# Keys' first part on ScalarE, row sums in halves, stores from another queue, output jobs placed later

## The chip, the cores and the metric

The kernel runs on one core of a Trainium2 chip, as one launch. The metric is the device time of that launch in microseconds (us), lower being better. Five engines work side by side, each through its own instructions in order: TensorE (PE), VectorE (DVE), ScalarE (ACT), GpSimd (POOL) and SyncE (SP), which here only issues DMA transfers. An instruction that waits holds up everything behind it on its engine. PE writes its results into PSUM banks, which other engines must empty before PE can use them again.

## The reference

```python
def _attn_ref(q, k, v, cap):                 # 4 batches, 12 heads, 448 rows, 64 wide
    scores = scale * np.matmul(q, k.transpose(0, 1, 3, 2))
    scores = cap * np.tanh(scores / cap)
    scores = scores - np.max(scores, axis=-1, keepdims=True)
    attn = np.exp(scores)
    attn = attn / (np.sum(attn, axis=-1, keepdims=True) + 1e-09)
    return np.matmul(attn, v)

def _moe_ref(x, modality_id, w_gate, modality_bias, w1, w2):   # 1792 x 768, 8 experts, 1024 wide
    logits = x @ w_gate + modality_bias[modality_id]
    e_idx = np.argmax(logits, axis=1)
    ...                                      # gate_w: the softmax weight of the chosen expert
    for e in range(E):
        mask = e_idx == e
        h = np.maximum(x[mask] @ w1[e], 0.0)
        out[mask] = gate_w[mask, None] * (h @ w2[e])

def _moe2_ref(x, w_gate, w_val, w_out):      # 768 -> 1536 -> 768
    gate = 1.0 / (1.0 + np.exp(-(x @ w_gate)))
    val = x @ w_val
    return gate * val @ w_out
```

The three run one after the other: attention, a layer in which each row goes to one expert, and a gated layer.

## The kernel before

All large products run in float16 with each operand split into a high part and a low part (the rest), so that three matmuls of parts stand for one product. Making the parts is work for ACT and DVE: `split_hi` (L923) copies the high part on ACT, line 928 subtracts it on DVE or POOL.

**Attention.** Heads are taken in pairs, six pairs a batch, 24 in all. A pair has four steps over keys (j = 0 to 3): `qk` makes scores, ACT takes tanh (L300) and exp (L305), `av` multiplies with values, and DVE adds up the rows for the sum (L325, L327, L333). The operands of the next pair are made beside it: `trans_k` in step 0 and `trans_q` in step 1 transpose on PE into a PSUM bank that `tr_tile` hands out. Then `parts_of` makes the high part (L259 on DVE, or L257 on ACT) and the low part (L260 on DVE), which frees the bank. Keys' parts are both made on DVE, queries' high part on ACT. One or two banks serve all these transposes and those of the ends of a batch, `end0g` to `end2`, L415 among them. Between them DVE converts weights of the gated layer for later (`conv_ops`, L862 to L864).

**Experts.** Rows are sorted into blocks of 128 by expert; the profile shows 15 blocks (540 matmuls at L730, 36 a block). Step s of the loop multiplies block s by w1 (`mm1`), applies relu on ACT (L734), transposes the result (`trh`, L709 on PE, L711 on ACT, L712 on DVE), multiplies block s-1 by w2 in two halves (`mm2`, L749), and takes that result out of its bank on ACT and DVE (`put_y`, L757, L758). A block of a new expert has its weights split by `split_w` (L689 on ACT, L693 on DVE) inside a branch, for w1 after relu (`split_new`) and for w2 after `put_y` (`next_w2`). A step has three places for other work, `fill[0]` to `fill[2]`. There go conversions of weights from `CV["raw"]` to `CV["cvt"]`, and in `fill[2]`, after `put_y`, the row sums: `y_sums(0, p)` makes for a tile of two blocks (p = 0 to 3) the sums of quarters that the seven-product scheme below needs. It returns four parts, a, b, d and e; DVE works at L975 to L1000, ACT copies the high part of each sum (L923), DVE makes the low one (L978). Tile 0's sums stand in step 9, those of tiles 1 and 2 in steps 10 and 11, inside a branch on the number of blocks (true here). After `fill[2]` come the jobs in `M["due"]`: from step 6 to 12 `set_keep` stores the two converted tiles from `CV["cvt"]` to DRAM (`keep`, L892, on SP's queue). The next step's conversions write those tiles again.

**The gated layer.** Each matrix product is made on two-by-two blocks with seven products instead of eight (Strassen's scheme in Winograd's form). The work has two halves (`sup` 0 and 1: eight and six tiles of 128 rows). In each, twelve sets of weights run through `gset`, then the output product runs in pieces of two tiles: p = 0 to 3 in the first half, 0 to 2 in the second. `z_job` makes a piece's seven operands: sums on DVE (`sums_of`, L901, two functions s1 and s2) and for each of the seven a high part on ACT and a low part on DVE (in the second half in turns on DVE and POOL), L920. Piece p+1's operands are made while piece p multiplies; `ZAT` and `ZBT` say after which product of that piece each job is issued, and `work` issues product and jobs in that order. A number past the last product means after the last.

A product is followed by what empties its bank (`opiece`). In `chain` four of the seven products add into one bank, one after the other, and after each ACT copies it (L1137). DVE adds the rest (L1140). In piece 0 and in the second half's last piece the seven have banks of their own (`seven`) and ACT copies one. A finished tile is sent to the output by an indirect DMA from POOL (L1126). The second half's rows come back through transposing DMAs on SP's queue (`y_load(1, ...)`, L966) into the space that pieces 0 and 1 read from. Their sums `y_sums(1, p)` run beside pieces 2 and 3 (`QC`, `QB`).

Of the kernel before, what the change touches and what calls it, by code (L numbers as in the profile page):

```python
# [57 lines left out]
WL = (0, 0, 0, 11, 25, 40)  # L58
FIRST = [(0, 1), (0, 2), (0, 7), (0, 6), (1, 1), (0, 5), (1, 2), (1, 6), (0, 3), (0, 4)]
QA = (6,) * 16  # L60
QB = (0, 1, 1, 2, 2, 3, 4, 4)
QC = (2, 3, 4, 5)
ZAT = (7, 7, 8, 8, 9, 9, 10, 10, 11)
ZBT = (0, 0, 0, 1, 1, 2, 3, 5, 6)

AFTER = ({'g0': 1, 'g1': 1, 's': 1, 'e1s': 4, 'e1g': 5, 'route': 6, 'route_b': 8, 'ga': 9, 'gb': 10, 'gc': 12, 'sc': (10, 12, 14, 16), 'e2': (7, 10, 12, 17, 21, 24), 'xw': (26, 27)}, {'g0': 1, 'g1': 1, 's': 1, 'e1s': 4, 'e1g': 5, 'route': 6, 'route_b': 10, 'ga': 9, 'gb': 10, 'gc': 12, 'sc': (10, 12, 14, 16), 'e2': (7, 10, 12, 17, 20, 23), 'xw': (26, 27)}, {'g0': 1, 'g1': 1, 's': 1, 'e1s': 5, 'e1g': 5, 'route': 6, 'route_b': 7, 'ga': 10, 'gb': 11, 'gc': 13, 'sc': (10, 11, 12, 13), 'e2': (6, 9, 10, 11, 12, 13), 'xw': (15, 15), 'ta': (9, 9), 'w1': (11, 11, 14, 12, 13, 13), 'w1s': (17, 18, 19, 23, 24, 24), 'w1l': (17, 18, 19, 26, 26, 26), 'idx': (11, 11), 'gather': (17, 18, 25), 'trx': (24, 25), 'w2': (20, 21, 26, 26)})

# [2 lines left out]
def tile_kernel(ctx: ExitStack, tc: tile.TileContext, q, k, v, cap, mod, wg, mb, w1, w2, gw, vw, ow, out, dbg=None):  # L70
    nc = tc.nc
# [176 lines left out]
    def tr_tile():  # L248

        M["trs"].append(M["trs"].pop(0))  # L250
        return bank(M["trs"][-1], "tr")

    def parts_of(dst, pt, n, eng):

        hi, lo = dst[:, 0], dst[:, 1]
        if eng is nc.scalar:
            nc.scalar.activation(out=hi, in_=pt[:, :n], func=AF.Copy, scale=SQ)  # L257
        else:
            eng.tensor_scalar(out=hi, in0=pt[:, :n], scalar1=SQ, scalar2=None, op0=ALU.mult)  # L259
        nc.vector.scalar_tensor_tensor(out=lo, in0=pt[:, :n], scalar=SQ, in1=hi, op0=ALU.mult, op1=ALU.subtract)  # L260

    def trans_k(g):

        b, i = divmod(g, NPAIR)
        t = kT[g] = att.tile([128, 2, 512], F16, name="kT")
        pt = tr_tile()
        for c in range(3):
            nc.tensor.transpose(pt[:, 128 * c:128 * c + 128], kf[g][:, c].rearrange("p h d -> p (h d)"), id32)
        nc.tensor.transpose(pt[:, 384:512], kt[b % 2][:, i], id32)
        parts_of(t, pt, 512, nc.vector)  # L270

    def trans_q(g):
        t = qT[g] = att.tile([128, 2, S], F16, name="qT")
# [560 lines left out]
    CV = {}  # L834
# [35 lines left out]
    def set_raw(s):  # L870
        for e in range(2):
            conv_load(*unit(s, e), CV["raw"][e])

    def wo_raw(i):
        for e in range(2):
            conv_load(2, 2 * i + e, CV["raw"][e])
# [4 lines left out]
    def g32_of(s, e):  # L881
        kind, j = unit(s, e)
        r = 128 * (12 * kind + j)
        return g32[r:r + 128, :]

    def set_keep(s):

        for e in range(2):
            keep(s, e)

    def keep(s, e):
        nc.sync.dma_start(out=g32_of(s, e), in_=CV["cvt"][e])  # L892

    def set_load(s, tiles):
        for e in range(2):
# [38 lines left out]
    def wo_job(t, w, to):  # L934

        s1, s2 = sums_of(False, t, w)
        ops = operands(False, t, w)
        hi, lo = splits([(ops[p], (to[:, p - 1, 0], to[:, p - 1, 1]), nc.vector) for p in (1, 2, 3, 5, 6, 7, 4)])
        return [s1, s2] + hi + lo
# [226 lines left out]
    with tc.manual_schedule():  # L1166
# [83 lines left out]
        for n in range(4 * NG + LAG):  # L1250
            g, j = divmod(n, 4)
# [111 lines left out]
            Z["wa"] = pool("wap", side="right").tile([128, 7, 2, 3, 128], F16, name="wa")  # L1363

        Z["ct"] = lambda s: CV["cvt"]
        M["due"] = []

        wst = [yr[:, c:c + 14 * 384].rearrange("p (q a n) -> p q a n", q=7, a=2) for c in (0, 12 * 512, 24 * 512)]
# [5 lines left out]
                    rest(s + 1)  # L1374

        YT = {8: 3, 9: 4, 10: 5, 12: 6, 13: 7}
        YS, YF = (9, 10, 11), (2, 2, 2)

        def y_more(p, cond):
            with tc.If(cond):  # L1380
                for f in y_sums(0, p):
                    f()

        def y_rest(tiles, cond):
# [3 lines left out]
        def conv_fill(fill, units):  # L1388

            c = [conv_ops(u[0], CV["raw"][e], CV["cvt"][e]) for e, u in enumerate(units)]  # L1390
            fill[0].extend(c[0][:3])
            fill[1].extend((c[0][3],) + c[1][:3])
            fill[2].append(c[1][3])

        for s in range(2, NFULL):
            fill = [], [], []
            i = s - WFILL
            if 0 <= i < NWO:
                conv_fill(fill, [(2, 2 * i + e) for e in range(2)])
                fill[1].append(lambda i=i: wo_raw(i + 1) if i + 1 < NWO else set_raw(early_sets[0]))  # L1400
                fill[2].extend(wo_job(halves(*CV["cvt"]), Z["w"], wst[i]))
            if 0 < i <= NWO:
                M["due"].append(lambda i=i: nc.sync.dma_start(out=wod[i - 1], in_=wst[i - 1].rearrange("p q a n -> p (q a n)")))
            if FILL <= s < FILL + len(early_sets):
                n = early_sets[s - FILL]
                conv_fill(fill, [unit(n, e) for e in range(2)])
                M["due"].append(lambda n=n: set_keep(n))
                if n != early_sets[-1]:
                    fill[1].append(lambda n=early_sets[s - FILL + 1]: set_raw(n))
                if n == 0:  # L1410
                    fill[2].extend(set_job(0, (nc.vector,) * 7))

            t = {5: 0, 6: 1, 7: 2}.get(s)
            if t is not None:
                fill[0].append(lambda t=t: y_load(0, (t,)))
            if s == YS[0]:
                fill[2].extend(y_sums(0, 0))
            if s == 6:

                nc.scalar.activation(out=M["glast"], in_=padc, func=AF.Sigmoid)  # L1420
            if s == 8:

                few = nc.values_load(tabs["b"][1][0:1, 0:1], engines=[ENG.SP], min_val=NFULL, max_val=NSLOT)
                fewv = nc.values_load(tabs["b"][1][0:1, 0:1], engines=[ENG.DVE, ENG.Activation, ENG.Pool], min_val=NFULL, max_val=NSLOT)
            for p in (1, 2):
                if s == YS[p]:
                    fill[YF[p]].append(lambda p=p: y_more(p, fewv < 16))
            t = YT.get(s)
            if t is not None:
                fill[0].append(lambda t=t: y_rest((t,), few < 16))  # L1430
            if s == 12:
                fill[0].append(lambda: y_rest((3,), few > 15))
            if s == 13:
                fill[2].append(lambda: y_more(1, fewv > 15))
            step(s, fill, more if s == 2 else None)
# [92 lines left out]

        def zjobs(sup, p, bufs, tmps, whole):
            j = z_job(sup, p, bufs, tmps, (DV, GP, DV, GP, DV, GP, DV) if sup else (DV,) * 7, allp, whole)  # L1530
            return list(zip(ZAT if p == 1 else ZBT, j))

        def work(calls, jobs):

# [7 lines left out]

            return [old[0], new[0], old[1], *new[1:], *old[2:]] if old else new

        pend = []
        for sup in range(2):
            nt = (4, 3)[sup]
            reg = (yr.bitcast(F32), zr)[sup]
# [3 lines left out]
            for s in range(12):  # L1552
                jobs = []
                if s < 11:
                    j = set_job(s + 1, LO[sup]) if sup or s else job
# [27 lines left out]
                pend = [prod(s, p) for p in (5, 7, 3, 4)]  # L1583
                work(calls, jobs)
            for p in range(nt):
                whole = p == 0 or sup and p == nt - 1
                jobs = []
                if p == 0:
                    jobs += [(6, f) for f in z_job(sup, 0, z0, zt, (DV,) * 7, slice(5, 6))]
                if sup == 0 and p == 2:  # L1590
                    Z["ct"] = lambda s: stg[2 * (s % 2):2 * (s % 2) + 2]
                    jobs += [(0, lambda: y_load(1, range(8, 14)))]
                    jobs += [(1, lambda: [set_load(s, Z["ct"](s)) for s in range(2)])]
                if p + 1 < nt:
                    jobs += zjobs(sup, p + 1, zbufs[p + 1], zt, sup and p + 1 == nt - 1)
                if sup == 0 and p == 2:
                    jobs += zip(QC, y_sums(1, 0))
                    jobs += zip(QA, set_job(0, (DV,) * 7))
                if sup == 0 and p == 3:
                    jobs += zip(QB, [f for i in range(1, 3) for f in y_sums(1, i)])  # L1600
                mm = opiece(sup, p, zbufs[p], whole)
                if p == 0:

                    calls = [lambda q_=q_, ks=ks, mm=mm: mm(q_, ks=ks) for ks in (range(5), range(5, 6)) for q_ in OORD]
                elif whole:
                    calls = [lambda q_=q_, mm=mm: mm(q_) for q_ in OORD]
                if whole:
                    calls = mixed(calls[:3], pend) + calls[3:]
                    pend = []
                else:  # L1610
                    calls = mixed([lambda q_=q_, mm=mm: mm(q_) for q_ in (1, 2, 6)], pend)
                    pend = [lambda q_=q_, mm=mm: mm(q_) for q_ in (5, 7, 3, 4)]
                work(calls, jobs)
# [40 lines left out]
```

## Time and profile before

| | us |
|---|---|
| median of 3 runs | 987.41 |
| lowest and highest run | 986.48, 987.56 |
| the profiled execution, its own time | 989.69 |
| its span, first to last instruction | 987.8 |
| PE busy in it | 922.4 |
| DVE, ACT, POOL busy | 710.2, 506.0, 172.3 |

The rows below come from that one execution. Its own time is 1.9 us more than its span. A row of a timeline has the start from the span's beginning, the duration, the engine, the line of the kernel, the operation, what is written from what, the shape, and how many instructions were merged into the row. In brackets stands how long the engine was idle before it and what ended that. "q" after an engine is its sequencer, which branches, waits and issues DMAs. "PE L749 <- DVEq L813" is a wait that DVE ended.

### The profile page before, as it was taken

Reading aid. Unit: us, or ns where it says so; the run is one execution under the profiler, and the core shown is the slowest. Engines: PE = TensorE matmul, PEld = TensorE weight load, DVE = VectorE, ACT = ScalarE, POOL = GpSimd, SP = SyncE. Lnnn points to the kernel's source line nnn. Section 1 sums busy time; section 2 is a strip of 40 time slices with the busy share of each in tenths; the row PEclk is TensorE's granted clock in tenths of the full one; section 3 lists DMA queues with packets and bytes.
Section 4 is the critical chain, followed back from the end, with each engine's and each line's share of the span. In section 5 each row is a group of like instructions: output and inputs, shape, how many; then the busy total and the mean of one; then the engine's idle time right before and its main releaser. Section 6 shows DMA issues by size and latency. Waiting matters only on the chain. (4 is left out here: it accounts for less than half of the span.)

```text
span 987.8 us, 14820 instructions
## 1 busy us (share of the span) xinstructions
PE 922.4 (93%) x5291; PEld 473.6 (48%) x5291; DVE 710.2 (72%) x1239; ACT 506.0 (51%) x817; POOL 172.3 (17%) x221
## 2 busy tenths in 40 slices
PE   6998989989898999989797999999989899999996
PEld 2333333333455555555355444444556556666554
DVE  4879888687774995387944899996698744545661
ACT  6978768658214663244532666544354345554330
POOL 4000000001011121111110000000010178883131
PEclk9999999989999999999999999999999999999999
DMA  5634464436347568759440555231062122220001
GB/s 137 168 99 113 115 189 117 124 101 230 129 126 301 187 220 267 235 171 373 161 130 20 159 197 181 96 117 43 17 126 83 65 96 81 79 67 1 1 33 64
DMA packets 119787, 128.78 MB, mean 130 GB/s; under 512 B 74464, under 2 KB 99952, under 8 KB 118928
## 3 DMA queue, kind: packets, MB, share of 16 engines
q1 hardware_dynamic: 114688, 107.83, 35.5%
q0 software_dynamic: 4208, 19.66, 5.8%
q8 instruction: 44, 0.72, 0.3%
q14 instruction: 47, 0.39, 0.1%
q10 hardware_dynamic: 800, 0.20, 0.1%
HBM read 91.16 MB, written 30.99 MB: 124 GB/s over the span
## 5 line engine op out<-in xcount | busy, mean ns | idle before, releaser
L1044 PEld LDWEIGHTS <-wa 128*128 128x128 f16 x909 | 89.6, 99 | 86.4 <-issue 8.3
L749 PE MATMUL sc<-w2s,hs 128*128 128x384 f16 x720 | 123.6, 329 | 6.8 <-DVEq L813 4.9
L730 PE MATMUL sc<-w1s,xT 128*128 128x512 f16 x540 | 120.0, 379 | 2.4 <-DVE w1s L693 1.5
L1044 PE MATMUL pp<-yr,wa 128*128 128x512 f16 (+1 forms) x468 | 101.3, 372 | 6.2 <-DVEq L1372 4.7
L749 PEld LDWEIGHTS <-hs 128*128 128x128 f16 x720 | 71.0, 99 | 49.6 <-ACT sta L865 5.2
L300 ACT ACTIVATE E<-sc,sct 128x896 f32<-128x896 f32 x72 | 72.4, 1006 | 41.5 <-PE sc L292 40.4
L730 PEld LDWEIGHTS <-xT 128*128 128x128 f16 x540 | 52.7, 98 | 64.4 <-issue 2.2
L1044 PE MATMUL pp<-zr,wa 128*128 128x384 f16 x441 | 75.7, 326 | 0.6 <-ACT yr L1092 0.6
L305 ACT ACTIVATE E<-E,capt 128x896 f32<-128x896 f32 x72 | 74.7, 1038 | 0.6
L314 PE MATMUL ot<-E,vf 128*64 128x448 f32 x288 | 70.3, 569 | 0.2 <-ACT E L305 0.2
L1044 PE MATMUL pp<-wos,yr 128*128 128x384 f16 x378 | 63.5, 331 | 5.7 <-ACT hs L1137 5.7
L901 DVE TENSOR_TENSOR sta<-sta 128x384 f32<-128x384 f32 x108 | 67.3, 663 | 2.0 <-DVE sta L901 0.5
L1126 POOL DMA_INDIRECT out_dram<-hs,pm x14 | 14.6, 1044 | 265.7 <-DVE hs L1140 198.7
L292 PE MATMUL sc<-qT,kT 64*128 64x448 f16 x432 | 56.1, 367 | 1.2 <-DVE kT L259 1.0
L1044 PEld LDWEIGHTS <-wb 128*128 128x128 f16 x378 | 37.0, 98 | 34.5
L1044 PEld LDWEIGHTS <-yr 128*128 128x128 f16 x378 | 37.5, 99 | 31.7 <-issue 8.1
L923 ACT ACTIVATE wa<-sta 128x384 f16<-128x384 f32 x98 | 48.6, 513 | 7.4 <-DVE sta L901 4.1
L1074 DVE TENSOR_TENSOR yr<-yr,pp 128x384 f32<-128x384 f32 x24 | 13.3, 553 | 46.4 <-PE pp L1044 46.4
L1044 PE MATMUL pp<-yr,wb 128*128 128x512 f16 x189 | 43.9, 379 | 0.0
L712 DVE TENSOR_TENSOR xT<-tr,xT 128x384 f16<-128x384 f32 x34 | 17.2, 551 | 34.7 <-ACT xT L711 34.3
L1024 PE MATMUL pp<-wos,sta 128*128 128x384 f16 x252 | 41.9, 326 | 0.0
L928 POOL TENSOR_TENSOR wa<-sta,wa 128x384 f16<-128x384 f32 x42 | 39.8, 965 | 6.0 <-ACT wa L923 6.0
(314 smaller groups left out, 1596.2 us busy)
## 6 DMA issues: line engine op xcount, KB each, us to landing
sta<-g SPq DMA_DIRECT2D x40, 384.0 KB, 3.1
st<-in_moe_w_dram SPq DMA_DIRECT2D x8, 1536.0 KB, 9.7
sta<-in_moe_w_out_dram SPq DMA_DIRECT2D x12, 768.0 KB, 4.4
sta<-in_moe_w_val_dram SPq DMA_DIRECT2D x12, 768.0 KB, 4.5
g<-sta SPq DMA_DIRECT2D x18, 384.0 KB, 4.4
qf<-in_q_dram SPq DMA_DIRECT2D x48, 112.0 KB, 3.9
vf<-in_v_dram SPq DMA_DIRECT2D x24, 192.0 KB, 2.9
st<-in_moe_w_gate_dram SPq DMA_DIRECT2D x6, 768.0 KB, 5.5
```

The costliest lines, as they stand in the source:

```text
L292: nc.tensor.matmul(sc[:, h, :S], kt_[p, a, 128 * j:128 * j + 128], qt_[p, b_], start=i == 0, stop=i == 2)
L300: nc.scalar.activation(out=e, in_=src, func=AF.Tanh, scale=sct)
L305: nc.scalar.activation(out=e, in_=e, func=AF.Exp, scale=capt)
L314: nc.tensor.matmul(ot[g][64 * h:64 * h + 64, :S], vf[g][:, h, j], e[:, h], start=j == 0, stop=False)
L712: nc.vector.tensor_tensor(out=lo, in0=pt[:, :128 * n], in1=hi, op=ALU.subtract)
L730: nc.tensor.matmul(p[:, nh], xT[s % 2][:, a, kk], w1s[:, b_, kk, 512 * nh:512 * nh + 512], start=i == 0, stop=i == 17)
L749: nc.tensor.matmul(M["p2"][:, nh, :384], hT[par][:, a, kk], w2s[:, b_, kk, 384 * nh:384 * nh + 384], start=i == 0, stop=i == 23)
L901: tt = lambda eng, o, x, y, op: eng.tensor_tensor(out=o, in0=x, in1=y, op=op)
L923: nc.scalar.activation(out=hi, in_=src, func=AF.Copy)
L928: los = [lambda x=x, d=d, e=e: e.tensor_tensor(out=d[1], in0=x, in1=d[0], op=ALU.subtract) for x, d, e in todo]
L1024: nc.tensor.matmul(bk[p][:, c0:c1], l(p, a, kk), r(p, b_, kk)[:, c0:c1], start=i == 0, stop=i == 3 * kn - 1)
L1044: nc.tensor.matmul(bk[c][:, c0:c1], l(p, a, kk), r(p, b_, kk)[:, c0:c1], start=i == c0 == 0 and p in (1, 2, 7), stop=i == 3 * kn - 1 and c ...
```

## The change

Four things change. `trans_k` has keys' high part made on ACT for the first five pairs of batches 1 to 3, 15 pairs. `keep` issues its stores from ACT's queue in the block loop, 14 stores. The row sums of tiles 0, 1 and 2 are cut in two, parts a and b in one step and d and e in the next, in steps 7 to 12 instead of 9 to 11; those of tiles 1 and 2 take two branches each. In the output stage, piece 1's second sums s2 are issued after piece 0's last product and the three jobs behind it (`carry`) after piece 1's first. Of piece 2's jobs the first three are issued after piece 1's first product and the other six after its third, behind the copy that follows that product. The row sums beside piece 3 start one product later.

```diff
-QB = (0, 1, 1, 2, 2, 3, 4, 4)
+QB = (1, 2, 2, 3, 4, 4, 5, 6)
 QC = (2, 3, 4, 5)
-ZAT = (7, 7, 8, 8, 9, 9, 10, 10, 11)
+ZAT = (7, 7, 8, 8, 9, 17)
 ZBT = (0, 0, 0, 1, 1, 2, 3, 5, 6)
+ZCT = (0, 0, 0, 2, 2, 2, 2, 2, 2)
...
-        parts_of(t, pt, 512, nc.vector)
+        parts_of(t, pt, 512, nc.scalar if b and i < 5 else nc.vector)
...
     def keep(s, e):
-        nc.sync.dma_start(out=g32_of(s, e), in_=CV["cvt"][e])
+        (nc.scalar if CV.get("own") else nc.sync).dma_start(out=g32_of(s, e), in_=CV["cvt"][e])
...
         Z["ct"] = lambda s: CV["cvt"]
+        CV["own"] = True
         M["due"] = []
...
-        YS, YF = (9, 10, 11), (2, 2, 2)
-
-        def y_more(p, cond):
+        YS = {7 + 2 * p + i: (p, slice(2 * i, 2 * i + 2)) for p in range(3) for i in range(2)}
+
+        def y_more(p, cond, which=slice(0, 4)):
             with tc.If(cond):
-                for f in y_sums(0, p):
+                for f in y_sums(0, p)[which]:
                     f()
...
-            if s == YS[0]:
-                fill[2].extend(y_sums(0, 0))
...
-            for p in (1, 2):
-                if s == YS[p]:
-                    fill[YF[p]].append(lambda p=p: y_more(p, fewv < 16))
+            if s in YS:
+                p, which = YS[s]
+                if p:
+                    fill[2].append(lambda p=p, which=which: y_more(p, fewv < 16, which))
+                else:
+                    fill[2].extend(y_sums(0, 0)[which])
...
             j = z_job(sup, p, bufs, tmps, (DV, GP, DV, GP, DV, GP, DV) if sup else (DV,) * 7, allp, whole)
-            return list(zip(ZAT if p == 1 else ZBT, j))
+            if p == 1:
+                carry.extend((0, f) for f in j[6:])
+            return list(zip(ZAT if p == 1 else ZCT if p == 2 else ZBT, j))
...
-        pend = []
+        pend, carry = [], []
...
-                jobs = []
+                jobs, carry[:] = carry[:], []
```

## Rows read from the trace of the kernel before

**Rows 1.** The page, busy time of each engine, share of the span, instructions.
```profile
PE 922.4 (93%) x5291; PEld 473.6 (48%) x5291; DVE 710.2 (72%) x1239; ACT 506.0 (51%) x817; POOL 172.3 (17%) x221
```

**Rows 2.** Timeline of all engines, 49 to 53 us, around one pair's keys.
```profile
49.31 0.67 ACT L305 ACTIVATE EM<-EM,capt 128x448 f32<-128x448 f32 x1
...
50.39 1.01 ACT L300 ACTIVATE E<-sc,sct 128x896 f32<-128x896 f32 x1 [0.42 <-PE sc L292]
...
50.85 0.68 DVE L259 TENSOR_SCALAR kT<-tr 128x512 f16<-128x512 f32 x1
...
51.56 0.69 DVE L260 SCALAR_TENSOR_TENSOR kT<-tr,kT 128x512 f16<-128x512 f32 x1
...
52.36 0.57 PE L276 MATMUL tr<-id,qf 112*128 112x112 f32 x4 [1.10 <-issue]
```

**Rows 3.** PE's timeline, 190 to 216 us: the last of the seven waits.
```profile
214.41 0.57 PE L276 MATMUL tr<-id,qf 112*128 112x112 f32 x4 [1.82 <-issue]
```

**Rows 4.** Who PE waited for, 440 to 545 us: total, times, longest.
```profile
PE sc L749 <- DVEq L813: 4.9, 1, 4.9
...
PE tr L709 <- ACTq L821: 4.2, 2, 2.5
```

**Rows 5.** PE's timelines of the two output stages: the waits for ACT.
```profile
724.20 8.94 PE L1044 MATMUL pp<-wos,yr 128*128 128x384 f16 x54 [1.13 <-ACT hs L1137]
735.09 32.34 PE L1044 MATMUL pp<-wos,yr 128*128 128x384 f16 x198 [1.95 <-ACT hs L1137]
770.06 22.25 PE L1044 MATMUL pp<-wos,yr 128*128 128x384 f16 x126 [2.64 <-ACT hs L1137]
...
938.51 8.94 PE L1044 MATMUL pp<-wos,zr 128*128 128x384 f16 x54 [2.12 <-ACT hs L1137]
```

**Rows 6.** Groups by line and shape: busy us, mean ns, idle before.
```profile
L711 ACT ACTIVATE hs<-tr 128x512 f16<-128x512 f32 x30 | 16.4, 599 | 22.3 <-PE tr L709 21.3 <-PE sc L749 0.9
...
L259 DVE TENSOR_SCALAR kT<-tr 128x512 f16<-128x512 f32 x24 | 16.4, 684 | 4.9 <-PE tr L269 4.9
```

**Rows 7.** Timelines of DVE, ACT and PE in steps 10 to 13.
```profile
449.72 1.03 DVE L975 TENSOR_TENSOR sta<-yr 128x384 f32<-128x384 f16 x2 [0.23 <-DVEq L813]
...
452.56 0.52 ACT L923 ACTIVATE yr<-sta 128x384 f16<-128x384 f32 x1 [0.66 <-DVE sta L988]
...
455.66 0.52 ACT L923 ACTIVATE yr<-sta 128x384 f16<-128x384 f32 x1 [1.05 <-DVE sta L1000]
...
458.88 4.06 PE L749 MATMUL sc<-w2s,hs 128*128 128x384 f16 x24
...
469.03 0.56 DVE L862 TENSOR_SCALAR sta<-sta 128x768 int32<-128x768 int32 x1 [2.46 <-DMA g<-sta]
...
476.31 5.74 PE L749 MATMUL sc<-w2s,hs 128*128 128x384 f16 x24 [4.94 <-DVEq L813]
...
488.60 7.93 PE L730 MATMUL sc<-w1s,xT 128*128 128x512 f16 x36
...
492.32 6.89 DVE L693 SCALAR_TENSOR_TENSOR w2s<-st,w2s 128x1024 f16<-128x1024 f32 x6
...
496.63 1.03 ACT L734 ACTIVATE hs<-sc 128x1024 f32<-128x1024 f32 x1 [0.21 <-PE sc L730]
...
500.92 1.04 PE L709 MATMUL tr<-id,hs 128*128 128x128 f32 x8
```

**Rows 8.** The stores at L892: issue and landing; SP's timeline at one pair.
```profile
L892 SPq DMA_DIRECT2D g<-sta x14: 319/378/853, 378.6 to 496.4; - x14
...
DMA to landing us min/median/max: 2.3/4.1/13.4
...
455.88 1.34 SPq L892 DMA_DIRECT2D g<-sta  x2
```

**Rows 9.** ACT's timeline in the first half's output stage.
```profile
734.57 0.47 ACT L1137 ACTIVATE hs<-pp 128x384 f32<-128x384 f32 x1
...
769.11 0.52 ACT L923 ACTIVATE zr<-sta 128x384 f16<-128x384 f32 x1 [3.20 <-DVE sta L983]
```

## The prediction

> **What bounds the kernel now.** I read the page first: TensorE (PE) is busy for 93% of the span [rows 1]. The reader is to see that no other engine is near it, so an edit is worth what it takes from PE's idle time. Then I read PE's timeline, which names before an instruction how long PE sat idle and what ended that, and the view of who waited for whom. Four places belong to this change. (a) Attention: seven times between 52 and 215 us PE waits until VectorE (DVE) has emptied a PSUM bank; the first and the last are shown [rows 2, 3]. (b) The loop over blocks, steps 10 to 13: PE waits 4.9 us once and 4.2 us in two waits [rows 4]. (c) The output stage of the first half: three waits for ScalarE (ACT) [rows 5]. (d) The same place in the second half: one [rows 5].
>
> **Attention: the first part of keys.** Fifteen of the 24 pairs move one 128x512 copy out of PSUM from DVE (0.684 us) to ACT, whose copy of that shape, on another line, takes 0.599 us [rows 6]. DVE then does only the second part, 0.69 us, after which the bank is free. In the first of the seven waits DVE starts the first part at 50.85, because older work was in front of it; the second part ends at 52.25, and PE goes on at 52.36 [rows 2]. ACT had nothing from 49.98 to 50.39, where it waited for PE; the copy fits there but for 0.599 - 0.42 = 0.18 us, which falls on the next tanh. So the second part can start at 50.85 and PE gains 0.68. Seven waits of this pattern give 7 x 0.68 = 4.8 us. For the other eight pairs I take nothing: there the bank is not what PE waits for. Bounds: above, all fifteen on PE's path, 15 x 0.68 = 10.3; below, nothing gained and 0.18 lost on each, 2.7. I take 4.8, by the traced waits.
>
> The Trainium skill ("ScalarE: Activation LUTs", section Rules for kernel authors) says of multiplies and the like: use VectorE, not ScalarE, as VectorE is faster per element. The rows differ for this PSUM source, 0.599 against 0.684 us [rows 6]. By the rule ACT's copy would be the longer one and outgrow the gap, this part would give nothing, and the time would be that of rival 1.
>
> **The block loop: row sums in halves, stores from ACT.** At the end of a step DVE makes one tile's row sums in four parts, with ACT copying the high half of each; ACT's next instruction is the relu of the next step, which PE's transposes need. The whole job runs from 449.72 to the end of its last ACT copy, 456.18; its first half ends for ACT at 453.08, so a half is 3.4 or 3.1 us [rows 7]. The stores now stand between it and the relu: two issues, 1.34 together as SP did a pair [rows 8].
>
> Step 10: relu comes 3.1 - 1.3 = 1.8 us earlier; of the 2.5 us wait [rows 4] 0.7 is left. Gain 1.8.
>
> Step 12: PE waits 4.9 us until DVE has taken an earlier block's result out of its bank. DVE is behind: it had waited for the sums of the step before, then 2.46 us for a store to leave its buffer [rows 7], which SP had issued behind a weight load. By the shorter sums the chain comes 1.8 us earlier, by a store that no longer queues on SP another 2.5: 0.7 is left, gain 4.2. After that wait 24 matmuls took 5.74 us against 4.06 elsewhere [rows 7]; I count the 1.7 as given back, since the long wait in front goes. The relu of this step is then late by as much as before or 0.2 more. Step 12: 4.2 + 1.7 - 0.2 = 5.7.
>
> Step 13 pays. It had no wait: relu at 496.63, transposes at 500.92, 12.3 us after the step's first matmul at 488.60 [rows 7]. Now the second half of the third tile's sums follows the split of a new expert's second weights, whose DVE part ends at 499.21, 10.6 after that matmul. With 0.23 for the branch, 3.1 for the half, 1.3 for two stores and 1.0 for relu that is 16.3 (16.5 with the 0.2 above), while PE is ready at 12.3. Loss 4.2. Before, that relu stood only behind ACT's part of the split.
>
> Sum of the loop: 1.8 + 5.7 - 4.2 = 3.3 us. Bounds: 7.5 with no new wait; -0.9 if the store's 2.5 and the 1.7 don't come. The other steps' stores I cost at nothing. DVE is free for such work 3.7 us after a step's first matmul (where the split begins, 492.32 against 488.60), and 3.7 + 0.23 + 3.4 + 1.3 + 1.0 = 9.6, so PE's readiness at 12.3 hides it by 2.7; without that cover each us is one of PE's.
>
> The trace shows the stores landing after 4.1 us in the median and 13.4 at most [rows 8]. The Trainium skill ("DMA: Bandwidth & Descriptors", section Issuing engines are not separate DMA queues) says that transfers started by different engines run on the same 16 DMA engines, so that another issuer saves only issue time. By it the store would land as late from ACT, and the sum would be that of rival 2.
>
> **The output stage.** In the first half's piece 0, ACT's copy that frees a bank is queued behind operand copies that wait for DVE's second sums; the change moves those sums to the end of the piece and the copies into the next one. PE's first wait, 1.13, goes. In piece 1 ACT's copy at 734.57 (0.47 us) comes behind copies of the next piece's operands [rows 9]; now these follow it. But the next product adds into the same bank, so the copy itself stays: 1.95 - 0.5 = 1.4. In piece 3 ACT's copy waits behind a row-sum copy that had itself waited 3.20 us for DVE [rows 9]; these jobs now start one product later, and 2.64 goes. Together 5.1. What is late next: DVE's additions go first, so piece 1's last operands come later, and with them the transposing loads on SP's queue, which overwrite what these jobs read, and the set loads behind. Their first reader is in piece 2, behind other DVE work; I cost this at nothing. If that cover is gone the third wait stays: 2.2 to 5.7.
>
> In the second half 2.12 goes [rows 5], less 0.2 as the next piece's copy gets more in front of it: 1.9 (0.9 to 2.1).
>
> **Sum.** 4.8 + 3.3 + 5.1 + 1.9 = 15.1 us. The profiled execution: span 987.8 - 15.1 = 972.7, with the 1.9 us around it 974.6. The median of the runs is 2.3 below that execution, 987.4; so 972.3.
>
> **Rivals.**
> 1. Keys' copies give nothing: ACT reaches them after tanh and exp, and DVE, in order, stands waiting for ACT. For it: ACT's gap is shorter than the copy. Against: in the seven DVE comes later still. 987.4 - 10.3 = 977.1. Here the change would not do what it says.
> 2. The loop gives back all: the stores land as late as before, so step 12 keeps its 2.5 and 1.7, while step 13 pays. For it: the load is in flight at that time. Against: the store no longer stands behind it in one queue. 15.1 - 3.3 - 0.9 = 10.9, so 976.5.
> 3. PE's waits in the output stage move instead of going, onto DVE's later jobs or the later loads; only 1.1 of the 5.1 stays: 976.3. For it: DVE's work there is not less, only placed elsewhere. Against: ACT's queue ended each of the three waits.
> 4. Slower: ACT is held by its stores. Each us (x) that an issue costs beyond 0.67 is 2 us in steps 10, 12 and 13, and in three more once 2.7 of cover are gone: 12x - 8.1. From x = 1.9, 2.6 us an issue, the whole gain is lost. If every store held ACT until it has landed, 4.1 us, x is 3.4 and 33 us are lost: 1005. For it: no row shows a store issued from ACT. Against: SP's took 0.38 in the median and 0.85 at most [rows 8].
>
> **Chances.** Forecast 0.52; rival 1 0.12, rival 2 0.16, rival 3 0.13, rival 4 0.07. A measurement of this kernel tells 0.2%, 2 us, from no change. The first four cases are faster, but two or three of the rivals together could come within that bound: faster 0.88, same 0.05, slower 0.07. The range takes in, below, about 6 us of the high ends of attention and the loop, and above, the rivals one by one or two of them together: 966.5 to 981.
>
> **What would show it.** Right: the seven waits in attention are some 0.7 us shorter, with ACT's copy ahead of DVE's second part; before step 12's second product a wait of at most 1.5 us, and 24 matmuls in about 4.1; a new wait of about 4 us before the transposes of step 13; of the four waits in the output stages only some 0.5 after piece 1. Wrong: stores on ACT's queue of over 1 us each; tanh starting late after the keys' copy; a wait for DVE or for a transposing load where ACT's stood.

## The result and the profile after

| | us |
|---|---|
| changed kernel, median of 5 runs (lowest, highest) | 976.14 (974.72, 977.79) |
| kernel before, median of 5 runs beside them | 987.46 (986.48, 988.67) |
| ratio, 95% interval | 0.9878, 0.9866 to 0.989 |
| profiled execution, its own time and its span | 977.14, 975.1 |
| PE busy in it | 920.8 |

The change takes 1.2% off: 11.3 us between the medians, 12.7 between the two spans (987.8 and 975.1). Forecast were 15.1 and 972.3 us; the time lies inside the range (966.5 to 981.0). Line numbers shift with the edits: in the changed kernel they are 2 or 3 higher than before (L257 is now L259, L749 is L752), in kernels 7 to 10 and 12 up to 4 (L753). The page of the changed kernel, busy time of each engine:

```profile
PE 920.8 (94%) x5291; PEld 473.1 (49%) x5291; DVE 700.7 (72%) x1224; ACT 512.4 (53%) x832; POOL 173.2 (18%) x221
```

PE has as many instructions as before and is busy 1.6 us less [rows 1]: 11.1 of the 12.7 us are idle time. To place the gain, I read from PE's two timelines when each stage's first matmul starts, and took differences. Those starts, before and after, are 242.76 and 237.13 (step 0), 425.83 and 419.66 (step 10), 445.68 and 437.12 (step 11), 462.77 and 454.22 (step 12), 488.60 and 473.55 (step 13), 505.69 and 493.94 (step 14), 527.65 and 515.62 (sets), 696.61 and 685.74 (output stage), 792.14 and 778.49 (sets, second half), 911.36 and 897.71 (its output stage).

| stage | before | after | gain | forecast |
|---|---|---|---|---|
| attention, to step 0's first matmul | 242.76 | 237.13 | 5.6 | 4.8 |
| steps 0 to 9 | 183.07 | 182.53 | 0.5 | 0 |
| step 10 | 19.85 | 17.46 | 2.4 | 1.8 |
| step 12 | 25.83 | 19.33 | 6.5 | 5.7 |
| step 13 | 17.09 | 20.39 | -3.3 | -4.2 |
| steps 11 and 14 | 39.05 | 38.78 | 0.3 | 0 |
| twelve sets of weights, first half | 168.96 | 170.12 | -1.2 | 0 |
| output stage, first half | 95.53 | 92.75 | 2.8 | 5.1 |
| sets, second half | 119.22 | 119.22 | 0.0 | 0 |
| output stage, second half | 76.42 | 77.36 | -0.9 | 1.9 |

So in these two executions the loop gave more than forecast and both output stages gave less, the second one less than nothing.

**Attention.** The timeline of the changed kernel at the first and the last of the seven places:

```profile
50.26 0.59 ACT L259 ACTIVATE kT<-tr 128x512 f16<-128x512 f32 x1
...
51.24 0.68 DVE L262 SCALAR_TENSOR_TENSOR kT<-tr,kT 128x512 f16<-128x512 f32 x1
...
51.98 0.60 PE L279 MATMUL tr<-id,qf 112*128 112x112 f32 x4 [0.34 <-DVE kT L262]
...
208.86 0.60 PE L279 MATMUL tr<-id,qf 112*128 112x112 f32 x4 [1.11 <-DVE kT L262]
```

ACT's copy runs while DVE is still at a conversion, and PE's wait is 0.34 where it was 1.10 [rows 2] and 1.11 where it was 1.82 [rows 3]. Over the seven places (1.10, 0.96, 1.00, 1.52, 1.00, 1.47 and 1.82 before) it fell from 8.9 to 3.8 us, by 0.47 to 0.82 each and 0.72 on average. Elsewhere PE waits longer for DVE: 0.84 where it was 0.17 in one place, and 1.74 in a place that had no wait:

```profile
205.52 0.65 PE L418 MATMUL tr<-id,OT 128*112 128x128 f32 x4 [1.74 <-DVE xr L419]
```

In all, PE's idle time up to step 0 fell by 4.4 us (25.1 to 20.7); the other 1.2 of the 5.6 is PE's busy time, which was that much shorter in this execution.

**The loop.** PE's timeline, steps 12 and 13 of the changed kernel; then DVE's and ACT's rows of step 13; then the view of the line that stores (issue time in ns, least, median, most; who waited; landing):

```profile
463.56 4.06 PE L752 MATMUL sc<-w2s,hs 128*128 128x384 f16 x24 [0.75 <-DVEq L816]
468.73 1.09 PE L712 MATMUL tr<-id,hs 128*128 128x128 f32 x8 [1.11 <-ACT hs L737]
...
489.11 1.09 PE L712 MATMUL tr<-id,hs 128*128 128x128 f32 x8 [3.06 <-ACT hs L737]
```

```profile
484.24 1.14 DVE L978 TENSOR_TENSOR sta<-sta,yr 128x384 f32<-128x384 f32 x2
...
487.17 0.81 ACTq L895 DMA_DIRECT2D g<-sta  x2
488.03 1.02 ACT L737 ACTIVATE hs<-sc 128x1024 f32<-128x1024 f32 x1 [0.56 <-ACT yr L926]
```

```profile
L895 ACTq DMA_DIRECT2D g<-sta x14: 326/346/477, 369.8 to 487.6; - x14
...
  DVE sta L865: 0.4, 1
...
DMA to landing us min/median/max: 2.3/3.3/6.9
```

The 4.9 us wait [rows 4] is 0.75, the matmuls behind it take 4.06 again, and step 13 has the new wait of 3.06. A pair of stores takes ACT 0.81, not 1.34. This trace has the landing of only five of the 14 stores.

**Output stages.** PE's timeline and then ACT's of the changed kernel, first and second half:

```profile
721.55 20.64 PE L1047 MATMUL pp<-wos,yr 128*128 128x384 f16 x126 [0.58 <-ACT hs L1140]
744.54 26.48 PE L1047 MATMUL pp<-wos,yr 128*128 128x384 f16 x162 [2.35 <-ACT hs L1140]
771.58 3.08 PE L1047 MATMUL pp<-wos,yr 128*128 128x384 f16 x18 [0.56 <-ACT hs L1140]
775.57 3.08 PE L1047 MATMUL pp<-wos,yr 128*128 128x384 f16 x18 [0.90 <-DVE hs L1143]
...
933.64 4.76 PE L1047 MATMUL pp<-wos,zr 128*128 128x384 f16 x18 [2.12 <-ACT hs L1140]
```

```profile
743.59 0.52 ACT L926 ACTIVATE zr<-sta 128x384 f16<-128x384 f32 x1 [2.15 <-DVE sta L991]
744.02 0.47 ACT L1140 ACTIVATE hs<-pp 128x384 f32<-128x384 f32 x1
...
932.37 0.84 ACT L926 ACTIVATE zr<-wa 128x768 f16<-128x768 f32 x1 [2.89 <-DVE wa L904]
933.12 0.47 ACT L1140 ACTIVATE hs<-pp 128x384 f32<-128x384 f32 x1
```

In the first half the waits of 1.13 and 2.64 are gone and 1.95 is 0.58 [rows 5], but a wait of 2.35 stands in piece 2, where there was none, and two short ones at the end. In the second half the wait of 2.12 before piece 1's first products is gone. But the next wait in that piece, three products on, has grown from 0.58 to 2.12 (that the lengths agree is chance), and 18 matmuls behind it take 4.76 us instead of 3.08. Before, that place read:

```profile
948.02 3.08 PE L1044 MATMUL pp<-wos,zr 128*128 128x384 f16 x18 [0.58 <-ACT hs L1137]
```

Both times ACT's copy out of the bank stands behind another copy that had waited for DVE. The windows of the second half in the changed kernel, all engines, with the granted clock behind the busy times:

```profile
927.00:933.00 6.00, 4.51 (x28) 2.60 (x27) 5.82 (x6) 3.08 (x5) 2.88 (x2) 1.00 0.21 82
933.00:941.00 8.00, 7.36 (x35) 4.01 (x35) 5.83 (x7) 4.74 (x8) 4.34 (x3) 0.79 0.01 2
```

After the wait the granted clock is 0.79 on average over 8 us, that is, part of them at 1.2 instead of 2.4 GHz.

### The profile page after: what moved, and what is told of

Its sections match the earlier page's. It is cut to its first block, busy times and chain, and to the rows that moved or that the text cites. A ratio compares the mean times of both kernels' runs of the same rounds, so it can differ in the third digit from the quotient of the medians.

```text
span 975.1 us, 14808 instructions
## 1 busy us (share of the span) xinstructions
PE 920.8 (94%) x5291; PEld 473.1 (49%) x5291; DVE 700.7 (72%) x1224; ACT 512.4 (53%) x832; POOL 173.2 (18%) x221
## 5 line engine op out<-in xcount | busy, mean ns | idle before, releaser
L752 PE MATMUL sc<-w2s,hs 128*128 128x384 f16 x720 | 122.0, 326 | 2.6 <-DVE w2s L696 1.9
L752 PEld LDWEIGHTS <-hs 128*128 128x128 f16 x720 | 70.5, 98 | 44.5 <-ACT sta L868 1.0
```

Source lines behind the costliest of these rows:

```text
L752: nc.tensor.matmul(M["p2"][:, nh, :384], hT[par][:, a, kk], w2s[:, b_, kk, 384 * nh:384 * nh + 384], start=i == 0, stop=i == 23)
```

## The experiments

Each kernel was timed in turns with the kernel before on one chip. "Gain" is the ratio times 987.5 us. The last three columns are lengths in that kernel's one profiled execution, by the starts in PE's timeline: from step 10's first matmul to the gated layer's first product, and the two output stages. Runs of one kernel spread by 1.6 to 8.2 us, and stretches at 1.2 GHz come in other places in each profiled execution, so a loop time of one execution is good to some 2.5 us (the changed loop took 95.7, 96.0 and 98.4 in three kernels); the output stages repeat far better.

| kernel | median | ratio, 95% interval | gain | loop | out 1 | out 2 |
|---|---|---|---|---|---|---|
| before | 987.46 | 1 | 0 | 101.8 | 95.5 | 76.4 |
| changed | 976.14 | 0.9878, 0.9866 to 0.989 | 12.0 | 96.0 | 92.8 | 77.4 |
| 1 keys alone | 983.83 | 0.9947, 0.9929 to 0.9966 | 5.2 | 102.3 | 95.3 | 76.4 |
| 2 halves and stores | 983.68 | 0.9967, 0.9955 to 0.9979 | 3.3 | 97.7 | 95.0 | 76.4 |
| 3 output jobs alone | 986.12 | 0.9975, 0.9965 to 0.9985 | 2.5 | 101.9 | 92.8 | 77.4 |
| 4 halves alone | 984.58 | 0.9967, 0.9955 to 0.998 | 3.3 | 98.9 | 93.8 | 76.4 |
| 5 stores alone | 989.74 | 1.0019, 1.0009 to 1.0028 | -1.9 | 104.0 | 95.1 | 76.4 |
| 6 changed, last half in step 13 | 971.07 | 0.9828, 0.9815 to 0.9841 | 17.0 | 93.6 | 92.8 | 77.4 |
| 7 changed, second half's output as before | 975.92 | 0.9871, 0.9856 to 0.9886 | 12.7 | 98.4 | 92.7 | 76.4 |
| 8 changed, one job later | 974.95 | 0.9872, 0.9857 to 0.9887 | 12.6 | 95.7 | 92.7 | 74.1 |
| 9 edits of 6 and 8 | 969.36 | 0.9799, 0.9776 to 0.9822 | 19.8 | 92.3 | 92.7 | 74.1 |
| 10 and row sums one product later | 969.62 | 0.9807, 0.9794 to 0.9819 | 19.1 | 92.6 | 92.5 | 74.1 |
| 11 changed, stores on SP | 977.07 | 0.9891, 0.9874 to 0.9907 | 10.8 | 99.0 | 92.7 | 77.3 |
| 12 as 9, stores on SP | 973.24 | 0.9842, 0.9822 to 0.9863 | 15.6 | 97.3 | 92.8 | 74.1 |

### 1. Keys alone

```diff
-        parts_of(t, pt, 512, nc.vector)
+        parts_of(t, pt, 512, nc.scalar if b and i < 5 else nc.vector)
```

> The kernel before with keys' high part on ScalarE and nothing else. Theory (DVE is late at the bank in seven places and loses one copy of 0.68 in each): 4.8 us faster by the prediction's sum, up to 5.6 by the start of the first block's product in the two traces; the time is 1 to 5 us under that of the kernel before if part of it is lost later, and PE's idle time in the seven places is some 0.7 us shorter each. Rival 1 (the copies on ScalarE give nothing): within 1 us of the kernel before, and the seven waits are as long as they were.

Measured: 5.2 us faster (3.4 to 7.0). The first and the last of the seven waits in PE's timeline of this kernel:

```profile
52.56 0.60 PE L276 MATMUL tr<-id,qf 112*128 112x112 f32 x4 [0.34 <-DVE kT L260]
...
209.47 0.60 PE L276 MATMUL tr<-id,qf 112*128 112x112 f32 x4 [1.11 <-DVE kT L260]
```

They are the waits of the changed kernel; the seven add up to 3.8 instead of 8.9, and the 1.74 us wait is there too. Rival 1 falls.

### 2, 4, 5. The loop's two edits, together and alone

Kernel 2 has the parts of the diff that concern `keep`, `CV["own"]` and `YS`; kernel 4 only those of `YS` and `y_more`; kernel 5 only the other two.

> The kernel before with the row sums in halves and the stores on ScalarE's queue, and nothing else. The prediction's sum says 3.3 us faster. The two traces say 5.9 to 6.4, because the wait in step 12 and its slow matmuls give 6.5 and step 13 takes only 3.3 back. Rival 2 (stores land as late, the loop gives everything back): 0.9 us slower, with the 2.46 us wait for a store still in front of a conversion on DVE.

> The kernel before with the row sums in halves, stores still on SP's queue. Tells the two loop edits apart. If the stores' queue matters as the prediction has it (2.46 us wait for a store behind a weight load, and 1.7 us of slow matmuls that follow), step 12 gets only the 1.8 us of shorter sums, step 10 gets 2.5, and step 13 pays 2 to 3: 1 to 3 us faster in all, 3 to 5 us behind the kernel with both edits. If the halves alone do it, it is as fast as the kernel with both edits, or up to 2 us faster, since no issue of 0.67 us stands in front of relu.

> The kernel before with the stores on ScalarE's queue and nothing else: row sums whole in steps 9 to 11 as before. If the place of the store is worth what the prediction took for it, step 12's wait shrinks from 4.9 to about 2.4 us and the slow matmuls behind it go, which is 4.2 less, while step 10's relu comes 1.3 later behind two issues: 2 to 3 us faster than before. If the kernel with halves alone (as fast as the one with both edits) is to be taken at its word, the store's place is worth nothing alone either: within 1 us of before, with step 12's wait moved behind relu.

Measured: 3.3 us faster, 3.3 faster, 1.9 slower. PE's timelines in steps 10 to 13, kernel 2, then 4, then 5:

```profile
467.46 4.06 PE L749 MATMUL sc<-w2s,hs 128*128 128x384 f16 x24 [0.31 <-DVEq L813]
473.26 1.09 PE L709 MATMUL tr<-id,hs 128*128 128x128 f32 x8 [1.74 <-ACTq L821]
...
493.50 1.35 PE L709 MATMUL tr<-id,hs 128*128 128x128 f32 x8 [2.92 <-ACT hs L734]
494.64 5.53 PE L749 MATMUL sc<-w2s,hs 128*128 128x384 f16 x24
```

```profile
471.38 6.74 PE L749 MATMUL sc<-w2s,hs 128*128 128x384 f16 x24 [4.81 <-DVEq L813]
...
496.14 1.09 PE L709 MATMUL tr<-id,hs 128*128 128x128 f32 x8 [0.92 <-ACTq L821]
```

```profile
439.89 1.97 PE L709 MATMUL tr<-id,hs 128*128 128x128 f32 x8 [3.03 <-ACT hs L734]
...
473.51 4.06 PE L749 MATMUL sc<-w2s,hs 128*128 128x384 f16 x24 [1.47 <-DVEq L813]
...
482.06 1.97 PE L709 MATMUL tr<-id,hs 128*128 128x128 f32 x8 [4.49 <-ACT hs L734]
```

Where a store leaves from decides which wait PE has. From SP (kernel 4), step 12's wait is the old one, 4.81, with 2.7 us of slow matmuls behind it, but relu is hardly late in step 13. From ACT (kernel 2), that wait is 0.31, and relu is late in steps 12 and 13. With whole row sums (kernel 5), the stores on ACT shrink step 12's wait too, to 1.47, but relu is late by 3.03 in step 10 and by 4.49 in step 12, and the kernel loses. My first expectation for kernel 5, 2 to 3 us faster, was wrong. I had taken step 12's shorter wait as a gain, but relu stays behind the whole row sums and one pair of issues (0.84 us), so that wait moved behind relu, as my second expectation said; its time, within 1 us of before, was missed by some 1 us. By the medians of kernels 2 and 4 the halves carry the gain, and the stores' place is worth nothing that can be measured.

### 11. The changed kernel with the stores back on SP

```diff
-        CV["own"] = True
```

> The changed kernel with the stores back on SP's queue, all else as changed. By the prediction (2.46 us wait for a store, 1.7 us of slow matmuls, against 1.3 us of issues in front of relu in steps 12 and 13): 2 to 4 us slower than the changed kernel, 978 to 980, with a wait of over 4 us in step 12 and one of 1 in step 13 in place of 3.06. If the two kernels with the loop edits alone are to be taken at their word (983.7 with the stores on ScalarE, 984.6 on SP), within 1 us: 975 to 977.

Measured: 1.3 us behind the changed kernel, with an uncertainty of some 2 (the two intervals), so neither expectation is excluded. PE's timeline:

```profile
463.30 5.58 PE L752 MATMUL sc<-w2s,hs 128*128 128x384 f16 x24 [5.42 <-DVEq L816]
...
487.44 1.09 PE L712 MATMUL tr<-id,hs 128*128 128x128 f32 x8 [1.47 <-ACTq L824]
```

The waits are those that the prediction's mechanism asks for: 5.42 and 1.5 of slow matmuls in step 12, and 1.47 in step 13, where the changed kernel has 0.75, 1.11 and 3.06.

### 6. The third tile's second half in step 13

```diff
-            if s in YS:
-                p, which = YS[s]
+            if s in YS and s < 12 or s == 13:
+                p, which = YS[min(s, 12)]
```

> The changed kernel with the second half of the third tile's sums in step 13 instead of 12, so that it no longer stands between the split of a new expert's second weights and relu. Theory (the 3.06 us wait before step 13's transposes is made by these sums and nothing else): that wait goes, step 14 takes it over only if DVE is late there too, which it is not in the trace: 3 us faster than the changed kernel, about 973. Rival (the work is only moved): the same wait appears in step 14 or before the gated layer's first product, and the time stays at 976.

Measured: 17.0 us faster than before, 4.9 more than the changed kernel (the intervals leave 3.2 to 6.7), against 3 expected. PE's timeline in step 13:

```profile
483.41 4.06 PE L752 MATMUL sc<-w2s,hs 128*128 128x384 f16 x24
487.31 1.04 PE L712 MATMUL tr<-id,hs 128*128 128x128 f32 x8
488.18 4.06 PE L752 MATMUL sc<-w2s,hs 128*128 128x384 f16 x24
```

There is no wait before any of them, step 13 takes 17.10 us as in the kernel before, and from step 14's first matmul to the gated layer it is 21.68 as in the changed kernel. So the 3.06 was made by these sums behind the weights' split, and one step later the same work costs nothing. By its length, 20.39 us in the changed kernel, step 13 accounts for 3.3 of the 4.9 us; where the rest of the median comes from is not shown (in this one execution step 12 was even 0.9 longer than in the changed kernel).

### 12. The stores' place once step 13 is free

Kernel 9 (below) without `CV["own"] = True`.

> The fastest kernel so far (third tile's second half in step 13, one operand job later; 969.4) with the stores back on SP's queue. Step 13 no longer waits there, so nothing is won back for relu by taking the issues off ScalarE. If the stores' place is worth what the waits in step 12 say (5.4 and 1.5 of slow matmuls with the stores on SP against 1.2 with them on ScalarE), this is 4 to 6 us slower, 973 to 975. If it is worth what the two pairs of kernels measured so far say (0 and 1.3), it is within 2 us: 969 to 971.

Measured: 15.6 us faster than before, 4.2 behind kernel 9 (the two intervals leave 1.2 to 7.3). PE's and then DVE's row in step 12:

```profile
466.29 5.54 PE L753 MATMUL sc<-w2s,hs 128*128 128x384 f16 x24 [5.41 <-DVEq L817]
```

```profile
459.01 0.56 DVE L866 TENSOR_SCALAR sta<-sta 128x768 int32<-128x768 int32 x1 [5.87 <-DMA g<-sta]
```

DVE waits 5.87 us for a store to leave its buffer. In kernel 9 it does not wait there, and PE's wait is 0.18. This is the cleanest test of the stores: where nothing is won back in step 13, ACT's queue is worth some 4 us, with the uncertainty above.

### 3. The output jobs alone

The parts of the diff that concern `QB`, `ZAT`, `ZCT` and `carry`.

> The kernel before with the output stage's jobs placed later and nothing else. The prediction's sum says 7.0 us faster (5.1 in the first half, 1.9 in the second). Rival 3 says 3.0 (1.1 and 1.9). The two traces say 1.9: 2.8 less in the first half, where a wait of 2.4 us in piece 2 takes the place of part of those removed, and 0.9 more in the second half, where the 2.12 us wait stays and 18 matmuls behind it run slower.

Measured: 2.5 us faster (1.5 to 3.5). That is rival 3's size and not the forecast's 7.0. The first output stage has 92.8 us and the second 77.4, as in the changed kernel.

### 7, 8, 9. The second half's output stage

Kernel 7 has `ZAT`, `ZBT` and no `carry` there, as before. Kernel 8 changes one number of the second half's last piece; kernel 9 is 6 and 8 together.

```diff
-            return list(zip(ZAT if p == 1 else ZCT if p == 2 else ZBT, j))
+            return list(zip(ZAT if p == 1 else ZC2 if sup and p == 2 else ZCT if p == 2 else ZBT, j))
...
+ZC2 = (0, 0, 2, 2, 2, 2, 2, 2, 2)
```

> The changed kernel with the second half's output stage as it was before (its jobs at the old places, nothing carried). By the prediction the new places are worth 1.9 us there, so this is 1.9 slower, about 978. By the trace of the changed kernel they cost 0.9, so this is 0.9 faster, about 975. The waits there should be 2.12 and 0.58 again.

> The changed kernel, with one job of the second half's last piece (the copy and subtraction that need its first sums) issued behind the third product instead of in front. Theory: in the trace PE's 2.12 us wait was for ScalarE's copy out of the bank, which stood behind this operand copy, which had itself waited 2.89 us for DVE; so the wait goes, and with it the slow matmuls that follow (1.7): 2 to 4 us faster than the changed kernel, 972 to 974. Rival (the copy waits for DVE's own later additions): the wait stays and the time is 976.

> The changed kernel with both of the last two edits: the third tile's second half in step 13, and the one operand job of the second half's last piece behind the third product. If they add, the time is that of the kernel with step 13's edit (971.1) less what the other is worth: 2.1 by the wait that its trace had lost, 3.8 with the slow matmuls, so 967 to 969. Rival (what the second edit gives is within the scatter of the clock, as its runs of 971.9 to 976.5 suggest): 970 to 971.

Measured: 0.7 and 0.6 us faster than the changed kernel, both within the intervals, so the medians of 7 and 8 tell nothing by themselves; that of 8 even leaves at most 2.5 of the 3.2 us by which its stage is shorter. 9 is 2.9 faster than 6 (0.3 to 5.5 by the two intervals). The stage tells more: 76.4 with the old places (waits of 2.12 and 0.58 again), 77.4 with the new, and 74.1 in every kernel that has the one job later (8, 9, 10 and 12). PE's timeline of kernel 8, the only wait that is left there:

```profile
929.78 3.08 PE L1048 MATMUL pp<-wos,zr 128*128 128x384 f16 x18 [0.58 <-ACT hs L1141]
```

The 2.12 and the slow matmuls went with the job that stood in front of ACT's copy. Kernel 9 has the lowest median, 969.36, and is 1.8 to 2.2% under the kernel before.

### 10. Row sums beside piece 2 one product later

```diff
-QC = (2, 3, 4, 5)
+QC = (3, 4, 5, 6)
```

> As the kernel with both edits, and the row sums beside piece 2 of the first half each one product later. Theory (the 2.35 us wait in piece 2, which stood in the place of two waits removed, is for ScalarE's copy behind the split of a row sum that waits for DVE): that wait goes, 2 us faster than the kernel with both edits. Rival 3 (DVE's work there is not less, so a wait only moves): the wait turns up in piece 3 or before the second half's first products, and the time is the same within 1 us.

Measured: the same time as kernel 9, and the first output stage takes 92.5 us instead of 92.7. PE's timelines there, kernel 9 and then 10:

```profile
739.97 34.02 PE L1048 MATMUL pp<-wos,yr 128*128 128x384 f16 x198 [2.35 <-ACT hs L1141]
```

```profile
739.90 11.86 PE L1048 MATMUL pp<-wos,yr 128*128 128x384 f16 x72 [0.29 <-ACT hs L1141]
752.57 14.79 PE L1048 MATMUL pp<-wos,yr 128*128 128x384 f16 x90 [0.81 <-ACT hs L1141]
768.72 3.08 PE L1048 MATMUL pp<-wos,yr 128*128 128x384 f16 x18 [1.37 <-ACT hs L1141]
772.72 3.08 PE L1048 MATMUL pp<-wos,yr 128*128 128x384 f16 x18 [0.91 <-DVE hs L1144]
```

The 2.35 us wait is 0.29, and 3.09 us of waits come behind it, where the changed kernel has 1.46 (0.56 and 0.90); the stage is as long as it was. My theory for this wait (ACT's order) was right about the place and wrong about the gain; rival 3 was right.

## Why the prediction held, and where it was wrong

**Attention: right.** Seven waits, 0.68 forecast and 0.72 measured for each. ACT's copy took 0.59 [rows 6: 0.599 on another line], and DVE's second part followed its older work without the first part between. Not forecast were the two waits that grew by 0.67 and 1.74; with them PE's idle time fell by 4.4 in all, less than the 5.0 of the seven. The Trainium skill ("ScalarE: Activation LUTs", section Rules for kernel authors) says to use VectorE and not ScalarE for a multiplication, which this pass is, and gives its factor of speed for bf16 alone. The trace does not agree for this f32 copy out of PSUM, 0.59 on ACT against 0.68 on DVE.

**The loop: right in its steps, too low in its sum.** All three signs came out. The term that was too high is the pair of issues in front of relu, 1.3 forecast and 0.81 measured: step 13's transposes came 15.6 us after its first matmul instead of 16.5, and PE was ready at 12.5, so 3.06 were lost instead of 4.2. In step 10 some 0.3 is left of the wait where 0.7 was forecast. The rows already had the better price: the median issue was 0.378 [rows 8], 0.76 a pair, and 1.34 was one slow pair. It accounts for 0.5 of the 0.6 to 0.9 us by which each of steps 10, 12 and 13 came out better. Together they gave 5.6 instead of 3.3. In medians the two edits by themselves gave 3.3 (2.1 to 4.4), as forecast and less than the 5.9 to 6.4 that I had read from the two traces; the larger figure is from single executions, which differ by 2.5 us there.

What the prediction had not seen is how the two edits act on each other in step 12. The halves alone bring DVE sooner to the buffer that a store still holds, so its wait there is longer and not shorter: 2.46 before [rows 7], 5.3 in kernel 4, 5.9 in kernels 11 and 12. The stores alone lose 1.9 us, because relu still stands behind whole row sums and now behind the issues too. That the pair is worth more than the halves shows only in kernels 9 and 12; kernels 2 and 4 have the same ratio, 0.9967.

**Rival 2: wrong in the loop's sum, and its reason fails in the landing times.** The pair that DVE waits for, issued in step 11, landed 13.1 and 13.4 us after its issue from SP before; recorded landings of the same pair are 13.5 to 13.9 in kernel 4 and 15.0 in kernel 11. From ACT they are 6.9 in the changed kernel, and 6.6 and 8.6 in kernel 2. The other stores landed about as late from either queue: the median of all 14 is 4.2 in kernel 2 and 4.4 before. The Trainium skill ("DMA: Bandwidth & Descriptors", section Issuing engines are not separate DMA queues) has another issuer save only issue time. The trace does not agree for this pair, which lands some 5 to 8 us sooner; the price of a pair of issues moved to ACT. That it had waited behind the weight load that SP had issued ahead is my reading and was not tested by itself.

**Rival 4** falls: issues from ACT took 0.48 us at most in the changed kernel and 1.39 once in kernel 6, and its point of decision was 2.6 for each.

**The first half's output: the step that failed is "their first reader is in piece 2, behind other DVE work; I cost this at nothing".** The two earlier waits shrank as forecast (1.13 to none, 1.95 to 0.58) and the third went. That sentence follows DVE's later jobs only as far as the loads behind them, and not to ACT's copies that wait for them. But the 2.5 us that PE gained in pieces 0 and 1 it waited in piece 2: ACT's copy at 744.02 stands behind the split of a row sum, for which ACT waited 2.15 us for DVE. It was not the transposing loads, but DVE's queue: in DVE's timeline the first sum of what they bring (zr) starts with no idle time in front of it, and in the windows DVE (third column of busy times) has 49.90 of 55 us.

```profile
738.54 1.02 DVE L978 TENSOR_TENSOR sta<-zr 128x384 f32<-128x384 f16 x2
```

```profile
721.00:776.00 55.00, 50.64 (x309) 30.20 (x309) 49.90 (x82) 25.05 (x47) 5.41 (x5) 1.00 0.43 108
```

What remains is the third wait, 2.64, and the slow matmuls behind it, less 0.56 and 0.90 at the end: 2.8 in all, between rival 3's 1.1 and the forecast's 5.1, and in the range of this part (2.2 to 5.7). Kernel 10 shows the reason: with ACT's order mended, the waits come out elsewhere and the stage is as long.

**The second half's output: the term "2.12 goes, less 0.2", forecast 1.9, measured -0.9.** The 2.12 went, as forecast; the term that was wrong is the 0.2. The next piece's jobs cost the next copy 1.54 us (0.58 to 2.12) and 1.68 more in the slow matmuls behind it. The carried jobs put four more DVE passes in front of the last piece's first sums, and the third job of that piece, in front of ACT's copy, needs these sums; ACT waited 2.89 us for them. I had costed the jobs that come in front by ACT's time for them and not by what they wait for. Kernel 8 shows it, since that one job behind the copy takes 3.2 us off the stage.

**What I had not forecast at all** is the 1.2 us lost in the first half's sets of weights. The granted clock around their start was 0.86 over 25 us, where the same stretch had 0.93 before; both follow a wait of PE at that place, 4.4 us and 4.7 before. This stage is the same work in all fourteen kernels, and its length is 168.5 to 170.2 us in their profiled executions. Kernel 8, which is the changed kernel up to the second half's last piece, took 168.5 where the changed kernel took 170.1, so this is scatter between executions; its cause was not tested.

So by the two profiled executions the total was near partly by luck, because errors with both signs met: attention +0.8, loop +2.3, other stages -0.4, output stages -5.1, together -2.4, which is 15.1 against 12.7. By the medians of kernels 1, 2 and 3 (5.2, 3.3 and 2.5, together 11.0, where the whole change gave 12.0) attention and loop came as forecast, and the miss is the 4.5 us of the output stages. Which of the two is nearer for the loop the runs cannot tell; both have the output stages wrong.

## What to carry to other kernels

A wait of PE for one engine is worth its length only if the engine behind that one is ahead of its own work: before a job is moved, ask for each instruction ahead of the copy that frees the bank what it waits for itself, not only how long it takes. Here, where the second engine was busy nine tenths of the stage, reordering the first only moved the wait (kernel 10). In the second half one job out of the way of the copy took 3.2 us off the stage, after the whole reordering had added 0.9 to it (kernel 8). Edits that each trade one wait for another, like the halves and the stores here, have to be measured together and apart: the stores lost 1.9 us alone, and were worth some 4 us beside the halves once the wait in step 13 had been moved.

## What was not expected of the hardware

A DVE addition of 0.95 us (128x768, f32) took longer while POOL worked on a subtraction. DVE's and POOL's rows of the changed kernel in the second half:

```profile
929.03 0.96 DVE L904 TENSOR_TENSOR wa<-yr 128x768 f32<-128x768 f32 x1
929.86 1.65 POOL L923 TENSOR_TENSOR zr<-yr,zr 128x768 f16<-128x768 f32 x1
930.10 2.24 DVE L904 TENSOR_TENSOR wa<-wa,yr 128x768 f32<-128x768 f32 x1
```

The second addition started 0.24 us into POOL's and took 2.24; it is one of the passes for which ACT's copy was late. In the kernel before, where this addition met no work of POOL, it took 0.96. All fourteen traces agree: 258 DVE passes of this kind and shape that shared at most 0.14 us with a POOL subtraction took 0.94 to 0.96, and the 22 that shared 1.4 to 1.6 us took 2.23 to 2.42 and ended some 0.8 us after POOL's. These 22 stand in two places of the program only, and no run moved POOL's work, so the cause is likely and not shown.

Also, after PE's waits of 2 to 5 us the next matmuls often ran slow, and often not: 24 of them took 6.74 behind a wait of 4.81 in kernel 4 and 5.58 behind 5.42 in kernel 11, while behind the 2.35 in the output stage of the changed kernel they ran at full speed. In step 13, behind waits of 3.06 and 3.08, 24 took 4.06 in the changed kernel and 6.05 in kernel 7. What decides it stays open.
